# Linear attention plus GELU block: another order and other buffers for the attention denominator and the output stage

## The chip, the core and the metric

The kernel runs on one core of one Trainium2 chip. The metric is the device time of one execution in microseconds (us). Before the change the median of three runs is 207.69 us (207.5 to 208.19).

## What is computed

The input x has 2048 tokens of 640 features (D), in bf16. The result is x + A(LN(x)) + B(LN(x)). B is a GELU layer with 1536 hidden features. A is linear attention with 32 heads of 20 features:

```python
phi = lambda t: jnp.where(t > 0, t + 1, jnp.exp(t)) + 1e-6
pq, pk = phi(q), phi(k)
kv = jnp.einsum("bhsd,bhse->bhde", pk, v)
z = jnp.einsum("bhsd->bhd", pk)
num = jnp.einsum("bhqd,bhde->bhqe", pq, kv)
den = jnp.einsum("bhqd,bhd->bhq", pq, z)[..., None] + 1e-6
o = num / den
return (lambda x, *d: x.transpose(*d))(o, 0, 2, 1, 3).reshape(B, S, D) @ wo
```

The denominator `den` is one number for each token and head. This case is about when and by which engines it is computed.

## The kernel before

A planner records instructions for each of the five engines in the order in which the code is run, and works out the semaphore waits from what each instruction reads and writes. Every engine then executes its own list in order; an instruction that waits holds up all behind it on that engine. A DMA is an entry in the list of the engine that issues it, so a DMA that waits holds up that engine's later entries as well. Before the change all DMAs apart from two at the start are issued by SyncE (SP).

The tokens are 16 tiles of 128, in four chunks of four tiles. PSUM has eight banks, which `take` (L190) hands out in rotation; a matmul group that takes a bank waits until the reader of that bank's earlier content is done.

The stages, in order of TensorE's list:

1. Layer norm, the transposed xn and the hidden layer HG of B (L365), to about 60 us of the profile.
2. K for all tiles and phi (L502, `phi`, L481), then the product of xn with phi(K) (L535). Meanwhile VectorE sums phi(K) over tokens, which gives z.
3. Q in four chunks (`q_chunk`, L543). For each of five blocks j TensorE makes one bank of Q (L547), ScalarE takes its exponential into a rotating buffer `ek` of three (L489), and VectorE does two instructions, a minimum (L490) and a combination (L492), the second of which reads the bank and writes PQ. "phi" below means these two on VectorE, and the second is the eviction of the bank. Between chunks 0 and 1 stands a small product (L561). In chunk 2 two matmul groups "MT" (L579) follow each Q block; ScalarE copies them (L585), and SyncE issues a DMA transpose of the result into Msb (L587).
4. Output, tile by tile: an accumulation of 12 products with W2 (24 matmuls of 320 columns, "W2 part") and 5 products of PQ with Msb (10 matmuls, "M part") into a pair of banks (both L659); then VectorE adds the bias to x (`xb`, L633), adds the bank pair (L678), and SyncE stores the tile (L681). `out_w2` and `out_fin` make the two parts. The last tile (`out_last`) is made in three pieces of 320, 192 and 128 columns, each with its own addition (L698) and store (L701).

The denominator of a chunk goes through five steps. `den_part` (L590): VectorE adds up the five blocks of PQ weighted with z ("sums", one instruction for each block, L593 and L596). `den_gather` (L600): four DMAs of 64 KB bring four partition groups together. `den_inv` (L607): VectorE adds these and takes the reciprocal. `den_spread` (L614): four DMAs bring the reciprocals to all partitions. `rden_scale` (L621): VectorE multiplies the five blocks of PQ. Only after that may an M part of that chunk start. The buffers of these steps lie in the memory of xn_tm, which is no longer read by then.

Before the change the sums of chunk 0 stand in Q chunk 1, one after each phi; its inverse stands in Q chunk 2, after block 3's MT; its spread is issued between chunks 2 and 3. The output stage begins with the W2 parts of tiles 0 to 3; beside them VectorE scales chunk 0, makes the sums of chunks 1 and 2, and the inverse of chunk 1. Then come the M parts of tiles 0 to 3, with the scaling of chunk 1 behind tile 1, and from tile 4 on the W2 part and the M part of one tile directly after one another.

Of the kernel before, what the change touches and what calls it, by code (L numbers as in the profile page):

```python
# [5 lines left out]
ALU = AluOpType  # L6
ACT = mybir.ActivationFunctionType
P = 128
FP32 = mybir.dt.float32
BF16 = mybir.dt.bfloat16  # L10
# [102 lines left out]
def bass_parallel_sum__linear_attn_block__dense_activation_gelu__prompt_kernel(  # L113
    nc: bass.Bass, A_x, A_wqkv, A_wo, B_x, B_w1, B_b1, B_w2, B_b2, out):
    Batch, S, D = A_x.shape
    F = B_w1.shape[1]
    assert Batch == 1 and D == 640 and F % P == 0 and S % 512 == 0
    NT = S // P
    CH = 4
# [4 lines left out]
    H = 32  # L124
# [13 lines left out]
    with contextlib.ExitStack() as es:  # L138
# [36 lines left out]
        free = xn_tm[:].rearrange("p t d -> p (t d)")  # L175
        MH = P // H
        SW = CW // MH
        yv = [free[:, 2 * CW * i:2 * CW * (i + 1)].bitcast(FP32) for i in range(NC)]
        y4 = [free[:, 2 * CW * (NC + i):2 * CW * (NC + i + 1)].bitcast(FP32).rearrange("p (m s) -> p m s", m=MH)
              for i in range(NC)]  # L180
        rdv = [free[:, 4 * CW * NC + CW * i:4 * CW * NC + CW * (i + 1)] for i in range(NC)]
        den_sb = sb("den_sb", [P, 2, SW], FP32)
        rden = sb("rden", [P, 2, SW], BF16)
        out_sb = sb("out_sb", [P, 2, D], BF16)
# [43 lines left out]
        r_M = [R_("M%d" % j) for j in range(DT)]  # L228
        r_MT = [[R_("MT%d_%d" % (j, h)) for h in range(2)] for j in range(DT)]
        r_zsum, r_zhl, r_z = R_("zsum"), R_("zhl"), R_("z")  # L230
        r_y = [R_("y%d" % c) for c in range(NC)]
        r_y4 = [[R_("y4_%d_%d" % (c, q)) for q in range(4)] for c in range(NC)]
        r_rdb = [[R_("rdb%d_%d" % (c, q)) for q in range(4)] for c in range(NC)]
        r_den, r_rden = [R_("den0"), R_("den1")], [R_("rden0"), R_("rden1")]
        r_out = [R_("out0"), R_("out1")]
# [243 lines left out]


        def phi(src, b, nb, dst, res_dst, extra_w):  # L481
            s = ring_e[0] % 3
            ring_e[0] += 1
            w = D if nb == 2 else CW
            et = ek[:, s, 0:w]
            e2 = halves(et) if nb == 2 else et
            d2 = halves(dst) if nb == 2 else dst
            br = B_[b:b + nb]
            Pl.ins("scalar", lambda e: e.activation(e2, src, ACT.Exp), reads=br, writes=[r_ek[s]])  # L489
            Pl.ins(v, lambda e: e.tensor_scalar(et, et, 1.0, 1e-6, ALU.min, ALU.add),  # L490
                   reads=[r_ek[s]], writes=[r_ek[s]])
            Pl.ins(v, lambda e: e.scalar_tensor_tensor(out=d2, in0=src, scalar=0.0, in1=e2,  # L492
                                                       op0=ALU.max, op1=ALU.add),
                   reads=br + [r_ek[s]], writes=[res_dst] + extra_w)

        ring_e = [0]
        for t in range(NT):
# [45 lines left out]
        def q_chunk(c, after=None):  # L543
            cc = slice(c * CW, (c + 1) * CW)
            for j in range(DT):
                b = take(1)
                Pl.ins("tensor", [(lambda e, k=k, j=j, b=b: e.matmul(  # L547
                    bank(b), Wqkv[:, k, j:D:DT], xnT[:, k, cc],
                    start=(k == 0), stop=(k == DT - 1))) for k in range(DT)],
                    reads=[r_Wq] + r_xnT[c * CH:(c + 1) * CH], writes=[B_[b]])  # L550
                phi(bank(b), b, 1, PQ[:, j, cc], r_PQ[c][j], [])
                if after:
                    after(j)
# [36 lines left out]
        def den_part(c, j):  # L590
            pq = PQ[:, j, c * CW:(c + 1) * CW]
            if j == 0:
                Pl.ins(v, lambda e: e.tensor_scalar(yv[c], pq, z_sb[:, 0:1], 1e-6 / MH, ALU.mult, ALU.add),  # L593
                       reads=[r_z, r_PQ[c][0]], writes=[r_y[c]] + r_xn)
            else:
                Pl.ins(v, lambda e: e.scalar_tensor_tensor(out=yv[c], in0=pq, scalar=z_sb[:, j:j + 1], in1=yv[c],  # L596
                                                           op0=ALU.mult, op1=ALU.add),
                       reads=[r_z, r_PQ[c][j], r_y[c]], writes=[r_y[c]])

        def den_gather(c):  # L600
            for q in range(MH):
                dst = y4[c][H * q:H * (q + 1)]
                src = yv[c][:, SW * q:SW * (q + 1)]
                Pl.ins("sync", lambda e, dst=dst, src=src: e.dma_start(dst, src),  # L604
                       reads=[r_y[c]], writes=[r_y4[c][q]], dma=True)

        def den_inv(c):  # L607
            s = c % 2
            Pl.ins(v, lambda e: e.tensor_reduce(out=den_sb[:, s, :], in_=y4[c].rearrange("p m s -> p s m"),
                                                axis=mybir.AxisListType.X, op=ALU.add),  # L610
                   reads=r_y4[c], writes=[r_den[s]])
            Pl.ins(v, lambda e: e.reciprocal(rden[:, s, :], den_sb[:, s, :]), reads=[r_den[s]], writes=[r_rden[s]])

        def den_spread(c):  # L614
            for q in range(MH):
                dst = rdv[c][:, SW * q:SW * (q + 1)]
                src = rden[H * q:H * (q + 1), c % 2, :].unsqueeze(1).to_broadcast([H, MH, SW])
                Pl.ins("sync", lambda e, dst=dst, src=src: e.dma_start(dst, src),  # L618
                       reads=[r_rden[c % 2]], writes=[r_rdb[c][q]], dma=True)

        def rden_scale(c):  # L621
# [10 lines left out]
        def xb(t):  # L632
            Pl.ins(v, lambda e: e.tensor_tensor(out=x_res[:, t, :], in0=x_res[:, t, :], in1=b2bc[:], op=ALU.add),  # L633
                   reads=[r_xr[t // CH], r_b2], writes=[r_xb[t]])
# [2 lines left out]
            x_again(c)  # L637
        q_chunk(0)
        kvt_step()
        q_chunk(1, lambda j: den_part(0, j))  # L640
        den_gather(0)

        def mt_and_den(j):
            mt_block(j)
            if j == 3:
                den_inv(0)
        q_chunk(2, mt_and_den)
        den_spread(0)
        q_chunk(3)

        r_out3 = R_("out3")

        def mm_ops(t, i):
            tok = slice(t * P, (t + 1) * P)
# [17 lines left out]
        def out_fin(t, b):  # L672
            s = t % 2
            for i in range(JT, JT + DT):
                Pl.ins("tensor", [mm(b, t, i, 0), mm(b, t, i, 1)], reads=mm_reads(t, i), writes=B_[b:b + 2],
                       mark=(i == JT + DT - 1))
            xb(t)
            Pl.ins(v, lambda e: e.tensor_tensor(out=halves(out_sb[:, s, :]), in0=pair(b),  # L678
                                                in1=halves(x_res[:, t, :]), op=ALU.add),
                   reads=B_[b:b + 2] + [r_xb[t]], writes=[r_out[s]])  # L680
            Pl.ins("sync", lambda e: e.dma_start(ov[t * P:(t + 1) * P, :], out_sb[:, s, :]),  # L681
                   reads=[r_out[s]], dma=True)

        def out_last(t):
            xb(t)
            lo = 0
            for i, w in enumerate((HW, 3 * 64, P)):
                b = take(1)
                o = out_sb[:, (0, 1, 0)[i], (0, 0, HW)[i]:(0, 0, HW)[i] + w]
                hs = slice(lo, lo + w)  # L690
                lo += w
                fns = []
                for q in range(JT + DT):
                    l, r = mm_ops(t, q)
                    fns.append(lambda e, l=l, r=r, q=q, b=b, hs=hs, w=w: e.matmul(  # L695
                        bank(b, 0, w), l, r[:, hs], start=(q == 0), stop=(q == JT + DT - 1)))
                Pl.ins("tensor", fns, reads=[r for q in range(JT + DT) for r in mm_reads(t, q)], writes=[B_[b]])
                Pl.ins(v, lambda e, b=b, hs=hs, w=w, o=o: e.tensor_tensor(  # L698
                    out=o, in0=bank(b, 0, w), in1=x_res[:, t, hs], op=ALU.add),
                    reads=[B_[b], r_xb[t]], writes=[r_out3 if i == 2 else r_out[i]])  # L700
                Pl.ins("sync", lambda e, hs=hs, o=o: e.dma_start(ov[t * P:(t + 1) * P, hs], o),  # L701
                       reads=[r_out3 if i == 2 else r_out[i]], dma=True)

        n_sync = len(Pl.records["sync"])
        bs = [out_w2(t) for t in range(4)]
        rden_scale(0)
        for c in (1, 2):
            for j in range(DT):
                den_part(c, j)
            den_gather(c)  # L710
        den_inv(1)
        den_spread(1)
        for t in range(4):
            out_fin(t, bs[t])
            if t == 1:
                rden_scale(1)
        den_inv(2)
        den_spread(2)
        for t in range(4, NT - 1):
            b = out_w2(t)  # L720
            out_fin(t, b)
            if t == 4:
                for j in range(DT):
                    den_part(3, j)
                den_gather(3)
            elif t == 5:
                rden_scale(2)
                den_inv(3)
                den_spread(3)
            elif t == 8:  # L730
                rden_scale(3)
        out_last(NT - 1)

        stores = [ev for (waits, fns, ev, dma) in Pl.records["sync"][n_sync:] if dma]
        for ev in stores[:-1]:
            Pl.wait_event("gpsimd", ev)
        Pl.wait_event("sync", stores[-1])
# [36 lines left out]
```

## Time and profile before

| what | us |
|---|---|
| median of three runs | 207.69 |
| the profiled execution | 207.95 |
| its span, first to last instruction | 206.5 |
| TensorE busy | 200.3 (97%) |
| VectorE busy | 127.1 (62%) |
| ScalarE busy | 73.7 (36%) |
| Q chunks, start of chunk 0 to start of the first W2 part | 103.40 to 129.62 |
| first W2 part to the last tile's first matmul | 129.62 to 199.50 |

The granted TensorE clock is 1.000 over the span. In the profile's lines, PE is TensorE's matmuls, PEld its weight loads, DVE is VectorE, ACT is ScalarE, SP is SyncE; an engine's name with a q is its queue, where DMAs are issued. A timeline line has the start in us, the length in us (of the whole group where several are merged), the engine, the line of the code, the operation, the tile written and the tiles read, the count, and in brackets the idle time of the engine before it with what ended it. A line of the waits has the waiting instruction, what it waited for, the total in us, the number of times and the longest.

### The profile page before, as it was taken

To read this page: it belongs to the slowest core of one execution; us is meant where nothing else is said; L and a number is where in the kernel's file an instruction comes from. 1 tells how busy PE (TensorE), PEld (TensorE's weight loads), DVE (VectorE), ACT (ScalarE), POOL (GpSimd) and SP (SyncE) were. 2 spreads that over 40 slices of the span, in tenths; PEclk is the share of its full clock that TensorE was granted. 3 is DMA by queue.
4 is the path that set the end of the run, shared out by engine and by line. 5 is a ranking of instruction groups with operands and counts; after the bars stand their busy time and mean duration, and the time that the engine had idled before them with its cause. 6 is when DMAs were issued, how large, how long until landed. Compare 5 with 4: busy or idle time off the path is not lost.

```text
span 206.5 us, 3787 instructions
## 1 busy us (share of the span) xinstructions
PE 200.3 (97%) x1490; PEld 137.9 (67%) x1497; DVE 127.1 (62%) x247; ACT 73.7 (36%) x141; POOL 14.5 (7%) x43
## 2 busy tenths in 40 slices
PE   6999999999999999999999979999999999999995
PEld 1799987444457777777756535677757777777775
DVE  4777677100007888999288989698769976323322
ACT  3589887666676455111153666100000000000000
POOL 3143434300000000000000000000000000000000
DMA  6993745499930000000395016301312213100002
GB/s 175 364 348 69 76 89 93 84 364 267 300 125 0 0 0 3 0 0 3 67 334 172 3 51 126 61 0 51 80 64 76 82 58 107 39 35 32 32 35 64
DMA packets 30696, 20.28 MB, mean 98 GB/s; under 512 B 16262, under 2 KB 30678, under 8 KB 30678
## 3 DMA queue, kind: packets, MB, share of 16 engines
q1 hardware_dynamic: 30382, 19.77, 34.5%
q10 hardware_dynamic: 296, 0.27, 0.4%
q8 instruction: 12, 0.20, 0.4%
q14 instruction: 6, 0.05, 0.1%
HBM read 12.72 MB, written 2.62 MB: 74 GB/s over the span
## 4 chain that ended last, share of the span: by engine, by line
PE 76%; DVE 11%; DMA 6%; SPq 3%; issue 2%; DVEq 0%; ACT 0%
PE ps L365 24%; PE ps L659 23%; PE ps L535 11%; PE ps L502 11%; DMA xn_tm<-rden 3%; DVE xn_tm L596 3%; PE ps L547 3%; DVE PQ L492 2%; PE ps L695 2%; DMA xn_tm<-xn_tm 2%; SPq L618 2%; SPq L604 2%; PE ps L397 1%; DMA xPK<-in_A_x_dram 1%; DVE PQ L624 1%
## 5 line engine op out<-in xcount | busy, mean ns | idle before, releaser
L659 PE MATMUL ps<-W,HG 128*128 128x320 bf16 x360 | 50.9, 299 | 0.0
L365 PE MATMUL ps<-xnT,W 128*128 128x256 bf16 (+2 forms) x382 | 50.4, 293 | 0.2
L365 PEld LDWEIGHTS ps<-xnT,W 128*128 128x128 bf16 x385 | 33.9, 98 | 15.9
L659 PEld LDWEIGHTS ps<-W,HG 128*128 128x128 bf16 x360 | 35.2, 98 | 13.8
L369 ACT ACTIVATE HG<-ps,b1c 128x256 bf16<-128x256 f32 (+2 forms) x77 | 38.0, 516 | 12.7 <-PE ps L365 10.3
L489 ACT ACTIVATE ek<-ps 128x512 bf16<-128x512 f32 (+1 forms) x36 | 23.2, 645 | 19.3 <-PE ps L502 9.2
L490 DVE TENSOR_SCALAR ek<-ek 128x512 bf16<-128x512 bf16 (+1 forms) x36 | 10.9, 303 | 26.9 <-ACT ek L489 25.7
L678 DVE TENSOR_TENSOR out_sb<-ps,xPK 128x640 bf16<-128x640 f32 x15 | 12.4, 825 | 19.8 <-PE ps L659 17.2
L659 PE MATMUL ps<-Msb,PQ 128*128 128x320 bf16 x150 | 22.6, 299 | 0.2 <-DVE PQ L624 0.2
L547 PE MATMUL ps<-xnT,Wqkv 128*128 128x512 bf16 x96 | 22.2, 379 | 0.2
L502 PE MATMUL ps<-Wqkv,xnT 128*128 128x320 bf16 x160 | 21.9, 299 | 0.0
L535 PE MATMUL ps<-xPK,xn_tm 128*128 128x320 bf16 x160 | 21.9, 299 | 0.0
L502 PEld LDWEIGHTS ps<-Wqkv,xnT 128*128 128x128 bf16 x160 | 15.7, 98 | 6.2
L535 PEld LDWEIGHTS ps<-xPK,xn_tm 128*128 128x128 bf16 x160 | 15.7, 98 | 6.1
L659 PEld LDWEIGHTS ps<-Msb,PQ 128*128 128x128 bf16 x150 | 14.3, 98 | 6.7 <-DVE PQ L624 1.4
L547 PEld LDWEIGHTS ps<-xnT,Wqkv 128*128 128x128 bf16 x100 | 11.3, 118 | 8.5
L321 DVE BATCH_NORM_STATS2 stats<-xPK 128x6 f32<-128x320 bf16 x32 | 14.7, 470 | 2.7 <-DMA xPK<-in_A_x_dram 2.7
L492 DVE SCALAR_TENSOR_TENSOR PQ<-ps,ek 128x512 bf16<-128x512 f32 x20 | 13.8, 692 | 2.1
L492 DVE SCALAR_TENSOR_TENSOR xPK<-ps,ek 128x640 bf16<-128x640 f32 x16 | 13.2, 824 | 1.7
L596 DVE SCALAR_TENSOR_TENSOR xn_tm<-PQ,z_sb,xn_tm 128x512 f32<-128x512 bf16 x16 | 12.0, 749 | 0.4
L522 DVE TENSOR_TENSOR Msb<-Msb,xPK 128x640 f32<-128x640 f32 x14 | 11.6, 825 | 0.5
L331 POOL TENSOR_TENSOR rstd<-aggr,mhalf 128x1 f32<-128x1 f32 x16 | 9.1, 568 | 15.7 <-DVE aggr L329 15.7
(56 smaller groups left out, 95.4 us busy)
## 6 DMA issues: line engine op xcount, KB each, us to landing
xPK<-in_A_x_dram SPq DMA_DIRECT2D x6, 640.0 KB, 7.5
Wqkv<-in_A_wqkv_dram SPq DMA_DIRECT2D x3, 800.0 KB, 6.9
out_dram<-out_sb SPq DMA_DIRECT2D x15, 160.0 KB, 1.8
W<-in_B_w_dram SPq DMA_DIRECT2D x1, 1920.0 KB, 15.0
W<-in_B_w_dram SPq DMA_DIRECT2D x2, 640.0 KB, 7.1
xn_tm<-xn_tm SPq DMA_DIRECT2D x16, 64.0 KB, 2.2
Wo<-in_A_wo_dram SPq DMA_DIRECT2D x1, 750.0 KB, 11.8
xPK<-in_A_x_dram SPq DMA_DIRECT2D x4, 160.0 KB, 4.5
```

Of the source, the lines that this page charges most:

```text
L321: Pl.ins(v, lambda e: e.bn_stats(stats[:, s, 6 * h:6 * h + 6], x_in[:, t, h * HW:(h + 1) * HW]), reads=[r_x[t]], writes=[r_stats[s][h]])
L365: Pl.ins("tensor", [(lambda e, k=k: e.matmul(bank(b, 0, w), W1[:, k, jb * P:(jb + 1) * P], xnT[:, k, tok], start=(k == 0), stop=(k == DT - ...
L369: Pl.ins("scalar", lambda e: e.activation(HG[:, jb, tok], bank(b, 0, w), ACT.Gelu_apprx_tanh, bias=b1c[:, jb:jb + 1]), reads=[B_[b], r_b1c ...
L489: Pl.ins("scalar", lambda e: e.activation(e2, src, ACT.Exp), reads=br, writes=[r_ek[s]])
L492: Pl.ins(v, lambda e: e.scalar_tensor_tensor(out=d2, in0=src, scalar=0.0, in1=e2, op0=ALU.max, op1=ALU.add), reads=br + [r_ek[s]], writes= ...
L502: fns.append(lambda e, k=k, h=h, b=b, t=t: e.matmul(bank(b + h, 0, HW), xnT[:, k, t * P:(t + 1) * P], Wqkv[:, k, D + h * HW:D + (h + 1) * ...
L522: Pl.ins(v, lambda e, t=t: e.tensor_tensor(out=zsum, in0=zsum, in1=PK[:, t, :], op=ALU.add), reads=[r_PK[t], r_zsum], writes=[r_zsum])
L535: Pl.ins("tensor", [(lambda e, t=t, h=h, b=b, f=f: e.matmul(bank(b + h, 0, HW), xn_tm[:, t, f * P:(f + 1) * P], PK[:, t, h * HW:(h + 1) * ...
L547: Pl.ins("tensor", [(lambda e, k=k, j=j, b=b: e.matmul(bank(b), Wqkv[:, k, j:D:DT], xnT[:, k, cc], start=(k == 0), stop=(k == DT - 1))) fo ...
L596: Pl.ins(v, lambda e: e.scalar_tensor_tensor(out=yv[c], in0=pq, scalar=z_sb[:, j:j + 1], in1=yv[c], op0=ALU.mult, op1=ALU.add), reads=[r_z ...
L659: return lambda e: e.matmul(bank(b + h, 0, HW), l, r[:, h * HW:(h + 1) * HW], start=(i == 0), stop=(i == JT + DT - 1))
L678: Pl.ins(v, lambda e: e.tensor_tensor(out=halves(out_sb[:, s, :]), in0=pair(b), in1=halves(x_res[:, t, :]), op=ALU.add), reads=B_[b:b + 2] ...
```

## The change

Five edits, made together:

- phi in the Q chunks takes its exponential buffers from eight in the memory of xn_tm instead of the three of `ek`. The buffers of the sums and gathers shrink from four to two, used in turn by chunk.
- The sums of chunk 0 are made in Q chunk 2, one after each block's MT, instead of in chunk 1. The gather follows chunk 2, the inverse stands in chunk 3 after block 3, and the spread is issued after chunk 3.
- In the output stage the W2 part of tile t + 2 is put right behind the M part of tile t, from t = 2 on. The sums, inverses, spreads and scalings of chunks 1 to 3 get other places, and the bias additions of tiles 0 to 3 are made ahead of the inverse of chunk 1.
- Of the gathers and spreads of chunks 1 to 3, every second DMA is issued by ScalarE instead of SyncE.
- The last tile is written to a buffer `out_l` of its own, not to the two buffers that the tiles use in turn. At the end GpSimd waits for the output stores alone; the list had the gathers and spreads in it as well.

```diff
+        rdv = [free[:, CW * (8 + i):CW * (9 + i)] for i in range(NC)]
+        NEQ = 8
+        ekq = [free[:, CW * (12 + i):CW * (13 + i)] for i in range(NEQ)]
...
         def phi(src, b, nb, dst, res_dst, extra_w):
-            s = ring_e[0] % 3
+            if nb == 2:
+                s = ring_e[0] % 3
+                et, re = ek[:, s, :], r_ek[s]
+            else:
+                s = ring_e[0] % NEQ
+                et, re = ekq[s], r_ekq[s]
...
         def den_part(c, j):
             pq = PQ[:, j, c * CW:(c + 1) * CW]
             if j == 0:
-                Pl.ins(v, lambda e: e.tensor_scalar(yv[c], pq, z_sb[:, 0:1], 1e-6 / MH, ALU.mult, ALU.add),
-                       reads=[r_z, r_PQ[c][0]], writes=[r_y[c]] + r_xn)
+                Pl.ins(v, lambda e: e.tensor_scalar(yv[c % 2], pq, z_sb[:, 0:1], 1e-6 / MH, ALU.mult, ALU.add),
+                       reads=[r_z, r_PQ[c][0]], writes=[r_y[c % 2]])
...
+        def dma_q(c, q):
+            return "scalar" if c and q % 2 else "sync"
...
-                Pl.ins("sync", lambda e, dst=dst, src=src: e.dma_start(dst, src),
+                Pl.ins(dma_q(c, q), lambda e, dst=dst, src=src: e.dma_start(dst, src),
...
-        q_chunk(1, lambda j: den_part(0, j))
-        den_gather(0)
+        q_chunk(1)
 
         def mt_and_den(j):
             mt_block(j)
-            if j == 3:
-                den_inv(0)
+            den_part(0, j)
         q_chunk(2, mt_and_den)
+        den_gather(0)
+        q_chunk(3, lambda j: den_inv(0) if j == 3 else None)
         den_spread(0)
-        q_chunk(3)
...
+        out_l = sb("out_l", [P, D], BF16)
...
-            xb(t)
+            if t >= CH:
+                xb(t)
...
-                o = out_sb[:, (0, 1, 0)[i], (0, 0, HW)[i]:(0, 0, HW)[i] + w]
                 hs = slice(lo, lo + w)
+                o = out_l[:, hs]
...
         bs = [out_w2(t) for t in range(4)]
+        den_parts(1, 0, DT)
+        den_gather(1)
         rden_scale(0)
-        for c in (1, 2):
-            for j in range(DT):
-                den_part(c, j)
-            den_gather(c)
+        for t in range(CH):
+            xb(t)
         den_inv(1)
         den_spread(1)
-        for t in range(4):
+        den_parts(2, 0, 1)
+        out_fin(0, bs[0])
+        den_parts(2, 1, 2)
+        out_fin(1, bs[1])
+        rden_scale(1)
+        for t in range(2, NT - 1):
             out_fin(t, bs[t])
-            if t == 1:
-                rden_scale(1)
-        den_inv(2)
-        den_spread(2)
-        for t in range(4, NT - 1):
-            b = out_w2(t)
-            out_fin(t, b)
-            if t == 4:
-                for j in range(DT):
-                    den_part(3, j)
+            if t == 2:
+                den_parts(2, 2, DT)
+                den_gather(2)
+            elif t == 4:
+                den_inv(2)
+                den_spread(2)
+            elif t == 5:
+                den_parts(3, 0, DT)
                 den_gather(3)
-            elif t == 5:
+            elif t == 6:
                 rden_scale(2)
+            elif t == 7:
                 den_inv(3)
                 den_spread(3)
-            elif t == 8:
+            elif t == 9:
                 rden_scale(3)
+            if t + 2 < NT - 1:
+                bs.append(out_w2(t + 2))
         out_last(NT - 1)
```

`den_parts(c, lo, hi)` makes the sums of the blocks from lo to hi - 1 of chunk c.

## The prediction

> **What bounds the kernel now.** I read the page's busy row and its 40 slices first, then the waits of TensorE, then the timelines of TensorE, VectorE and SyncE around each wait, and last the end of the span. The page's rows for TensorE and its weight loads:
>
> ```profile
> PE 200.3 (97%) x1490; PEld 137.9 (67%) x1497; DVE 127.1 (62%) x247; ACT 73.7 (36%) x141; POOL 14.5 (7%) x43
> ...
> PE   6999999999999999999999979999999999999995
> ```
>
> TensorE is busy nearly all the time; after the first microseconds only slice 24 (118.7 to 123.9 us) and the last slice dip. So an edit in the attention denominator can gain only what TensorE loses to waits, plus something at the end. The waits of TensorE:
>
> ```profile
> PE ps L579 <- DVE PQ L492: 1.3, 1, 1.3
> ...
> PE ps L659 <- DVE PQ L624: 0.2, 1, 0.2
> ```
>
> The two left out lie before 7 us, which the change does not touch. These rows say 1.46 us. Here a rule of the Trainium skill speaks (Trainium Kernel Development and Optimization, Performance Expectations): matmul busy time is a bad metric, since matmuls are pipelined; weight-load busy is the better one. Weight loads at 67% would suggest a third of the span as room. The rows don't bear that out: 96 matmuls of 320 columns of the W2 stage start within 13.04 us (129.62 to 142.66), 136 ns each, and a load takes 98 ns of each interval, 72% with nothing idle. [...] I measure each from start to start. The timeline of TensorE:
>
> ```profile
> 121.38 0.23 PE L579 MATMUL ps<-W,Wo 120*128 120x120 bf16 x2 [1.29 <-DVE PQ L492]
> 121.45 1.25 PE L547 MATMUL ps<-xnT,Wqkv 128*128 128x512 bf16 x5
> 122.54 0.45 PE L579 MATMUL ps<-W,Wo 120*128 120x120 bf16 x6
> 122.84 1.25 PE L547 MATMUL ps<-xnT,Wqkv 128*128 128x512 bf16 x5
> ...
> 148.10 3.42 PE L659 MATMUL ps<-W,HG 128*128 128x320 bf16 x24
> 151.69 1.79 PE L659 MATMUL ps<-Msb,PQ 128*128 128x320 bf16 x10 [0.17 <-DVE PQ L624]
> 153.31 3.42 PE L659 MATMUL ps<-W,HG 128*128 128x320 bf16 x24
> 156.57 1.52 PE L659 MATMUL ps<-Msb,PQ 128*128 128x320 bf16 x10
> 157.93 3.42 PE L659 MATMUL ps<-W,HG 128*128 128x320 bf16 x24
> ```
>
> First wait, Q chunk 2: one step (a Q block and its two MT groups) takes 1.38 us undisturbed (Q blocks start at 116.97 and 118.35). The fourth Q block should start at 119.73 and starts at 121.45: **1.72 us** lost. Second, tile 4: W2 part to M part takes 3.59 instead of 3.26 us, and the M part 1.62 instead of 1.36: 0.33 + 0.26 = **0.59 us**.
>
> VectorE and ScalarE at the first wait:
>
> ```profile
> 118.88 0.69 DVE L492 SCALAR_TENSOR_TENSOR PQ<-ps,ek 128x512 bf16<-128x512 f32 x1
> 119.49 0.74 DVE L596 SCALAR_TENSOR_TENSOR xn_tm<-PQ,z_sb,xn_tm 128x512 f32<-128x512 bf16 x1
> ...
> 120.54 0.69 DVE L492 SCALAR_TENSOR_TENSOR PQ<-ps,ek 128x512 bf16<-128x512 f32 x1
> ```
>
> The banks rotate over 8. In chunk 2 each step takes three (Q, MT a, MT b), so MT b of step j takes the bank of Q block j-2, and MT a of step 2 that of chunk 1's last. These evictions end at 119.57 and 121.23, and TensorE goes on at 119.72 and 121.38, 0.15 us after each. VectorE is late because in chunk 1 it takes 1.66 us a step (113.51 to 115.17, phi plus a sum) while TensorE makes a Q block in 1.08.
>
> **The change, part by part.**
>
> *Sums of chunk 0 move from chunk 1 to chunk 2.* Chunk 1 is then phi alone: 1.00 us (121.14 to 122.14), inside TensorE's 1.08. So VectorE enters chunk 2 on time: chunk 1's last exp starts at 115.80, its eviction ends near 117.52, and the first exp of chunk 2 ends at 117.48. From 117.52 the steps take 1.40 with the first sum (112.11 to 113.51) and then 1.66; an eviction ends 1.08 after its step starts. Evictions of blocks 0, 1, 2 end at 118.6, 120.0, 121.66. MT b of steps 2, 3, 4 would like to start at 119.64, 121.02, 122.40 and may from 118.75, 120.15, 121.81. The narrowest slack is 0.59 us: the whole 1.72 us go. Bounds: a sum at its full 0.74 instead of 0.66 us moves the last by 0.16, still nothing; if chunk 2's steps (ScalarE copying MT from PSUM beside them, a mix that no row shows with sums) cost 0.4 more, the loss is about 0.3. A gain beyond 1.72 is excluded, as nothing but that wait is there. I take 1.72, range 1.4 to 1.72.
>
> *Eight exp buffers in Q.* ScalarE's waits for a buffer are 0.5 us in all, one time, and TensorE doesn't wait for them. VectorE will end chunk 2 at 117.52 + 1.40 + 4 x 1.66 = 125.56, some 2 us behind, less than the three steps that three buffers cover. 0 either way.
>
> *Chunk 0's gather, inverse, spread come later.* SyncE: the five transposes of chunk 2 (1.23 us each) are now ahead of the gather; the last is ready near 123.8, issued by 125.1, so they hold nothing. Gather from 125.6, landing 4.2 later (120.26 to 124.45): 129.8. VectorE meanwhile does four phis of chunk 3 to 129.6, waits 0.2, and takes 2.03 for the inverse (124.57 to 126.60): 131.9. The fifth phi waits behind it, to 132.9; its bank is wanted by W2 of tile 3 at 137.7 at the earliest, so that hides it. Spread: 5.1 us from inverse to landing (146.02 to 151.11): 137.0. The sums of chunk 1 (3.55, 136.12 to 139.67) run to 136.45 beside it, and the scaling of chunk 0 (1.77) ends at 138.8. The M part of tile 0 is due at 129.62 - 1.72 + 13.04 = 140.94. Cover 2.1 us: 0 lost, range 0 to 0.5.
>
> *Head of the output stage.* Behind that VectorE has four bias additions (0.53 each) to 140.9, the inverse of chunk 1 to 142.95, one sum (0.41), then the first output addition (0.82) to 144.2. M parts of tiles 0 to 2 take 3 x 1.36, so W2 of tile 4, in tile 0's banks, is due at 145.02: slack 0.8. This is the tightest place of the new order. Scaling of chunk 1: spread from 142.95, landing 148.05 at the latest, done 149.8; its first reader, the M part of tile 4, is due at 145.02 + 3.26 + 1.36 + 3.26 = 152.9, because W2 parts now stand ahead. So the 0.59 us go. Same sum for chunk 2: done near 166, wanted at 171.4; chunk 3: near 180, wanted at 190. 0 lost; range 0 to 1.
>
> *Gather and spread on two queues.* Each issue takes 0.60 us of SyncE's time, so two fewer behind one another save 1.2 of a gather's 4.2 us. A rule of the Trainium skill (DMA: Bandwidth & Descriptors, Issuing engines are not separate DMA queues) is against hoping for more: all issues run on the same DMA engines and interleave, only issue time is saved. By the row alone chunk 1's gather lands at 136.5 + 3.0 = 139.5; if interleaving ate even that, 140.7. VectorE is at its additions until 140.9, so the sum gets 0 from either. ScalarE's own issues (0.62 and 0.41 at the start) lie where it has no other work.
>
> *Own buffer for the last tile.* The timeline of the end:
>
> ```profile
> 204.06 0.33 SPq L701 DMA_DIRECT2D out_dram<-out_sb  x1
> ...
> 204.36 0.29 DVE L698 TENSOR_TENSOR out_sb<-ps,xPK 128x128 bf16<-128x128 f32 x1
> ...
> 204.91 0.43 SPq L701 DMA_DIRECT2D out_dram<-out_sb  x1
> ```
>
> The waits put 2.6 us before the first two of the three additions to tile 14's store, but the third still starts when TensorE ends. The cost is on SyncE: the last store issues at 204.91, though its data is there at 204.65 and an issue follows some 0.1 later. Without the pile: 204.75, so **0.15 us**; bounds 0 and 0.25. GpSimd's final waits are now for output stores alone: 0, since it ends with the stores as before.
>
> Sum: 1.72 + 0.59 + 0.15 = 2.46 us. The profiled execution took 207.95 us (span 206.5): 205.49. The median of the runs, 207.69, lies 0.26 lower, so 205.2.
>
> **The rivals.**
>
> *Part of the wait comes back* (VectorE slower in chunk 2, or the first output addition late): for it speaks the 0.59 and 0.8 of slack, less than one phi; against it that all durations are of the same shapes. Up to 1.4 us lost: 205.6 to 206.6.
>
> *The change doesn't do what it says in chunk 2*: the weight load's wait is put to ScalarE's MT copies (1.43), and if those were the cause the 1.72 stays: 207.69 - 0.74 = 206.95. The copies end by 119.3, long before 121.34, while both restarts follow an eviction by 0.15: unlikely.
>
> *Slower: the inverse of chunk 1 blocks VectorE.* It stands ahead of tile 0's addition in VectorE's order and waits for the gather on two queues. If that lands late, the addition, tile 0's banks and W2 of tile 4 all slip by it. It costs from 140.9 + 0.8 = 141.7 on, and makes the kernel slower once it eats the 2.46 as well, at 144.2: 7.7 us after its issue, against 4.2 in the trace. At 9 us: 207.69 + 1.3 = 209. For it: no gather on ScalarE's queue is in the trace. Against: that queue's start-up load of 256 KB landed in 4.0 us, and the DMA engines are 17% busy in this stretch (129.6 to 142.6).
>
> **How the numbers follow.** A measurement of this kernel tells about 0.3%, 0.6 us, from no change. The forecast, 205.2 (204.8 to 205.6): 0.70. Part of the wait back: 0.10. The first wait stays: 0.05, of which I count 0.03 as faster. Slower: 0.11. Cancelling losses within 0.6 us: 0.04. Faster 0.83, same 0.06, slower 0.11. The range takes the first two: 204.7 to 206.6.
>
> **What would show it.** TensorE's row for MT waiting on L492 is gone and chunk 2 keeps its 1.38 us a step; W2 begins near 127.9; every W2 part follows its M part at 3.26 and 1.36 us; the waits of the scalings are VectorE's alone; the last store issues within 0.15 us of the last addition. I am wrong if TensorE shows a new wait on an output addition (tile 4), on a scaling (tile 0), or if MT still waits in chunk 2.

## The result, and the profile after

The changed kernel takes 205.34 us (median of 4 runs, 205.16 to 205.5), where the kernel before took 207.81 in runs beside it (207.5 to 208.19). The ratio is 0.988, with a 95% interval of 0.986 to 0.990: 2.5 us less, with 2.46 forecast. The profiled execution took 205.16 us, its span is 203.8 us, and the granted TensorE clock is 1.000 as before.

The page's busy row and the slices of TensorE:

```profile
PE 200.1 (98%) x1497; PEld 138.4 (68%) x1497; DVE 126.9 (62%) x247; ACT 73.5 (36%) x141; POOL 14.5 (7%) x43
...
PE   7899999999999999999999999999999999999996
```

The busy times are those of before: no work went away. The dip that stood in slice 24 is gone. The waits of TensorE are down to these two, both before 6 us:

```profile
PE ps L311 <- DVE warm L281: 1.3, 1, 1.3
PE ps L389 <- DVE xn_tm L382: 0.6, 1, 0.6
```

The timeline of TensorE shows the places of both waits. L585 is the MT group, L553 the Q block, L669 the output stage:

```profile
120.80 0.45 PE L585 MATMUL ps<-W,Wo 120*128 120x120 bf16 x6
121.10 1.25 PE L553 MATMUL ps<-xnT,Wqkv 128*128 128x512 bf16 x5
122.19 0.45 PE L585 MATMUL ps<-W,Wo 120*128 120x120 bf16 x6
122.48 5.57 PE L553 MATMUL ps<-xnT,Wqkv 128*128 128x512 bf16 x25
127.88 13.20 PE L669 MATMUL ps<-W,HG 128*128 128x320 bf16 x96
140.92 4.24 PE L669 MATMUL ps<-Msb,PQ 128*128 128x320 bf16 x30
145.00 3.42 PE L669 MATMUL ps<-W,HG 128*128 128x320 bf16 x24
148.26 1.52 PE L669 MATMUL ps<-Msb,PQ 128*128 128x320 bf16 x10
```

Read the starts. The last Q block of chunk 2 starts at 121.10 and the first of chunk 3 at 122.48, 1.38 later, an undisturbed step. W2 begins at 127.88 instead of 129.62: 1.74 us. Three M parts then take 4.08, a W2 part 3.26, and no start in the stage is late. The last tile begins at 197.16 instead of 199.50, 2.34 us earlier, so the second wait gave 0.60. The timelines of SyncE and VectorE at the end:

```profile
201.46 0.33 SPq L712 DMA_DIRECT2D out_dram<-out_l  x1
...
202.02 0.29 DVE L709 TENSOR_TENSOR out_l<-ps,xPK 128x128 bf16<-128x128 f32 x1 [0.59 <-PE ps L706]
...
202.34 0.33 SPq L712 DMA_DIRECT2D out_dram<-out_l  x1
```

The last store is issued 0.03 us after its data is there (202.31), where it was 0.26 before, and the issue takes 0.33 instead of 0.43. From the end of the last addition to the end of the span it is 1.49 us instead of 1.85: 0.36. The three terms, 1.74 + 0.60 + 0.36, are the 2.7 us between the spans (206.5 and 203.8) of these two executions; the medians differ by 2.5.

### The profile page after: what moved, and what is told of

Same layout as the page of the kernel before. It is cut to its first block, busy times and chain, and to the rows that moved or that the text cites. A ratio compares the mean times of both kernels' runs of the same rounds, so it can differ in the third digit from the quotient of the medians.

```text
span 203.8 us, 3769 instructions
## 1 busy us (share of the span) xinstructions
PE 200.1 (98%) x1497; PEld 138.4 (68%) x1497; DVE 126.9 (62%) x247; ACT 73.5 (36%) x141; POOL 14.5 (7%) x43
## 4 chain that ended last, share of the span: by engine, by line
PE 96%; DVE 1%; DMA 1%; issue 0%; DVEq 0%
PE ps L669 34%; PE ps L368 25%; PE ps L541 11%; PE ps L508 11%; PE ps L553 11%; PE ps L706 2%; PE ps L400 1%; DMA xPK<-in_A_x_dram 1%; DVE stats L324 1%; PE ps L567 1%; PE ps L585 1%; PE ps L389 0%; PE ps L352 0%; DVE xn_tm L382 0%; DVE out_l L709 0%
## 5 line engine op out<-in xcount | busy, mean ns | idle before, releaser
L669 PE MATMUL ps<-W,HG 128*128 128x320 bf16 x360 | 50.9, 299 | 0.0
L669 PEld LDWEIGHTS ps<-W,HG 128*128 128x128 bf16 x360 | 35.2, 98 | 13.8
L553 PE MATMUL ps<-xnT,Wqkv 128*128 128x512 bf16 x100 | 22.8, 379 | 0.0
L669 PE MATMUL ps<-Msb,PQ 128*128 128x320 bf16 x150 | 22.3, 299 | 0.0
L496 DVE TENSOR_SCALAR ek<-ek 128x640 bf16<-128x640 bf16 x16 | 5.2, 325 | 26.0 <-ACT ek L495 24.8
L669 PEld LDWEIGHTS ps<-Msb,PQ 128*128 128x128 bf16 x150 | 14.7, 98 | 5.7
L553 PEld LDWEIGHTS ps<-xnT,Wqkv 128*128 128x128 bf16 x100 | 11.3, 118 | 8.5
L495 ACT ACTIVATE xn_tm<-ps 128x512 bf16<-128x512 f32 x20 | 11.9, 597 | 9.4 <-PE ps L553 8.7
L498 DVE SCALAR_TENSOR_TENSOR PQ<-ps,xn_tm 128x512 bf16<-128x512 f32 x20 | 13.8, 692 | 2.1
L495 ACT ACTIVATE ek<-ps 128x640 bf16<-128x640 f32 x16 | 11.3, 704 | 9.2 <-PE ps L508 9.2
```

Source lines behind the costliest of these rows:

```text
L553: Pl.ins("tensor", [(lambda e, k=k, j=j, b=b: e.matmul(bank(b), Wqkv[:, k, j:D:DT], xnT[:, k, cc], start=(k == 0), stop=(k == DT - 1))) fo ...
L669: return lambda e: e.matmul(bank(b + h, 0, HW), l, r[:, h * HW:(h + 1) * HW], start=(i == 0), stop=(i == JT + DT - 1))
```

## The experiments

Each ran in five rounds beside the kernel before. Ratios are to that kernel.

**One part alone: the sums of chunk 0 in chunk 2.** On the kernel before:

```diff
-        q_chunk(1, lambda j: den_part(0, j))
-        den_gather(0)
+        q_chunk(1)
 
         def mt_and_den(j):
             mt_block(j)
-            if j == 3:
-                den_inv(0)
+            den_part(0, j)
         q_chunk(2, mt_and_den)
+        den_gather(0)
+        q_chunk(3, lambda j: den_inv(0) if j == 3 else None)
         den_spread(0)
-        q_chunk(3)
```

> The kernel before with one part alone: chunk 0's sums in Q chunk 2, its gather behind chunk 2, its inverse in chunk 3 and its spread behind it; three exp buffers, one queue, the old output stage. My theory (TensorE's waits follow VectorE's order): the first wait goes, W2 begins 1.74 us earlier, at 127.9. But in the old output stage VectorE then scales chunk 0 to 138.1, makes ten sums to 145.3, gets chunk 1's gather near 146.0, and does tile 0's addition only near 149.3, where W2 of tile 4 is due at 146.4: 3.1 us lost there, and about 1.2 more at the M part of tile 4 for chunk 1's scaling, in place of 0.59 before. Sum: -1.74 + 4.3 - 0.59 = +2.0, so 209.8 us, slower. Rival (the parts add up, each with its own gain): 207.8 - 1.7 = 206.1 us.

Measured: 209.72 us, ratio 1.0088 (1.0055 to 1.0122). Slower, near my 209.8. Three of the six runs had a granted clock of 0.992; the median of the other three is 209.64, so the clock is not the cause. The timeline of TensorE of this kernel, at full clock:

```profile
127.92 13.20 PE L658 MATMUL ps<-W,HG 128*128 128x320 bf16 x96
140.96 5.60 PE L658 MATMUL ps<-Msb,PQ 128*128 128x320 bf16 x40
148.98 3.43 PE L658 MATMUL ps<-W,HG 128*128 128x320 bf16 x24 [2.43 <-DVE out_sb L677]
153.11 1.78 PE L658 MATMUL ps<-Msb,PQ 128*128 128x320 bf16 x10 [0.69 <-DVE PQ L624]
154.73 3.42 PE L658 MATMUL ps<-W,HG 128*128 128x320 bf16 x24
```

W2 does begin 1.7 us earlier, and all of it is lost again at tile 4. Its W2 part would be due at 140.96 + 4 x 1.36 = 146.40 and starts at 148.98: 2.58 lost. Its M part comes 4.13 later instead of 3.26 and takes 1.62 instead of 1.36: 1.13 more. Together 3.71, where this tile lost 0.59 before: 3.12 more, less the 1.7 won, so TensorE comes out 1.4 us behind the old trace, less than the 2.0 that I had put together. (This execution was the fastest of the six.) The timeline of VectorE tells why:

```profile
136.07 1.77 DVE L624 TENSOR_TENSOR PQ<-PQ,xn_tm 128x512 bf16<-128x512 bf16 x5 [3.09 <-DMA xn_tm<-rden]
137.75 0.48 DVE L593 TENSOR_SCALAR xn_tm<-PQ,z_sb 128x512 f32<-128x512 bf16 x1
138.27 3.11 DVE L596 SCALAR_TENSOR_TENSOR xn_tm<-PQ,z_sb,xn_tm 128x512 f32<-128x512 bf16 x4
141.30 0.48 DVE L593 TENSOR_SCALAR xn_tm<-PQ,z_sb 128x512 f32<-128x512 bf16 x1
141.82 3.11 DVE L596 SCALAR_TENSOR_TENSOR xn_tm<-PQ,z_sb,xn_tm 128x512 f32<-128x512 bf16 x4
145.63 1.03 DVE L609 TENSOR_REDUCE den_sb<-xn_tm 128x128 f32<-128x512 f32 x1 [0.70 <-DMA xn_tm<-xn_tm]
146.70 0.95 DVE L612 RECIPROCAL rden<-den_sb 128x128 bf16<-128x128 f32 x1
147.57 0.43 DVE L633 TENSOR_TENSOR xPK<-xPK,b2bc 128x640 bf16<-128x640 bf16 x1
148.10 0.82 DVE L677 TENSOR_TENSOR out_sb<-ps,xPK 128x640 bf16<-128x640 f32 x1
```

The scaling of chunk 0, ten sums, an inverse that waits for its gather and a bias addition stand ahead of tile 0's addition, which alone frees the banks for W2 of tile 4. It ends at 148.92. The same list stood there in the kernel before, with this addition:

```profile
146.47 0.82 DVE L678 TENSOR_TENSOR out_sb<-ps,xPK 128x640 bf16<-128x640 f32 x1
```

It ended at 147.29, 0.81 before W2 of tile 4 started at 148.10. With the sums in chunk 2 that list begins 1.6 later, as its scaling waits for a later spread (136.07 instead of 134.44), and TensorE comes 1.7 earlier. The parts of the change do not add up: this one pays only with the other order behind it.

**The new output stage alone**, on the kernel before, all DMAs on SyncE: the diff of the change from `bs = [out_w2(t) ...]` on, and the bias additions. Core:

```diff
         bs = [out_w2(t) for t in range(4)]
+        den_parts(1, 0, DT)
+        den_gather(1)
         rden_scale(0)
-        for c in (1, 2):
-            for j in range(DT):
-                den_part(c, j)
-            den_gather(c)
+        for t in range(CH):
+            xb(t)
         den_inv(1)
         den_spread(1)
...
```

> The kernel before with the new output stage alone (places of sums, inverses, spreads, scalings and bias additions, W2 parts two tiles ahead), all DMAs on SyncE, chunk 0's sums still in chunk 1. My theory: the first wait of 1.72 us stays, the second of 0.59 us goes: 207.2 us. Rival (the new order only pays behind an early W2 start, or one queue makes chunk 1's spread late): 207.8 us or above, with a wait of W2 or M of tile 4 in the trace.

Measured: 207.34 us, ratio 0.9966 (0.9948 to 0.9985), 0.3 to 1.1 us less. In its trace the 1.29 us wait of MT stands as before and W2 begins at 129.56; from there to the M part of tile 5 no start is late. The 0.6 us of the second wait are this part's own.

**The last tile's buffer alone**, on the kernel before:

```diff
+        out_l = sb("out_l", [P, D], BF16)
...
-                o = out_sb[:, (0, 1, 0)[i], (0, 0, HW)[i]:(0, 0, HW)[i] + w]
                 hs = slice(lo, lo + w)
+                o = out_l[:, hs]
...
```

> The kernel before with the last tile's own buffer alone. The two traces give 0.26 us from the last data to the issue of the last store before and 0.03 after, and an issue of 0.43 before and 0.33 after, so 0.15 to 0.33 us: 207.5 to 207.65. Rival (the final waits of GpSimd or the landing set the end): no change, 207.8.

Measured: 207.88 us, ratio 1.0001 (0.9981 to 1.0021). The runs can't tell 0.3 us, and can't exclude it. The trace has the effect: 1.55 us from the end of the last addition (204.85) to the end of the span (206.4), against 1.85 before. But in this profile TensorE reaches the last tile at 199.70 instead of 199.50, from a later start of work that the edit doesn't touch: the first MT starts at 116.94 instead of 116.68, and over the traces of all runs at 116.63 to 117.08. Such shifts between executions are as large as the term. So the 0.3 us are seen in traces, and not shown in times.

**The W2 parts not two tiles ahead**, on the kernel after:

```diff
         for t in range(2, NT - 1):
+            if t >= 4:
+                bs.append(out_w2(t))
             out_fin(t, bs[t])
...
-            if t + 2 < NT - 1:
-                bs.append(out_w2(t + 2))
```

> The kernel after, but the W2 part of tile t from 4 on directly ahead of its own M part, as before the change; the places on VectorE, SyncE and ScalarE relative to the M parts unchanged. My theory now: VectorE's order is what ended the wait at tile 4. Chunk 1's scaling ends at 146.7, and the M part of tile 4 would be due at 149.6 in this order too: no wait, 205.3 us. Rival, as the prediction put it (the W2 parts that stand ahead cover the scaling): the wait comes back in part, up to 0.6 us, 205.9 us.

Measured: 205.57 us, ratio 0.9885 (0.9857 to 0.9913); no difference from the kernel after that the runs can tell. The timelines of TensorE and VectorE of this kernel:

```profile
146.41 3.42 PE L669 MATMUL ps<-W,HG 128*128 128x320 bf16 x24
149.66 1.52 PE L669 MATMUL ps<-Msb,PQ 128*128 128x320 bf16 x10
151.02 3.42 PE L669 MATMUL ps<-W,HG 128*128 128x320 bf16 x24
```

```profile
144.99 1.76 DVE L633 TENSOR_TENSOR PQ<-PQ,xn_tm 128x512 bf16<-128x512 bf16 x5 [0.24 <-DMA xn_tm<-rden]
```

The M part of tile 4 is due 3.3 us earlier than in the kernel after, at 149.66, and starts then: chunk 1's scaling is done at 146.75. The old order of TensorE loses nothing. What ended the second wait is VectorE's order in the output stage; in the kernel with the first part alone, which keeps the old order there, the wait grew to 1.13.

**All DMAs on SyncE**, on the kernel after:

```diff
-            return "scalar" if c and q % 2 else "sync"
+            return "sync"
```

> The kernel after with all gathers and spreads issued by SyncE. My theory: each gather and spread of chunks 1 to 3 lands up to 1.2 us later, and VectorE has other work or TensorE has slack (W2 of tile 4 due at 145.0, tile 0's addition done at 143.3; chunk 1's scaling done at 146.7, wanted at 152.9): no change, 205.3 us. Rival (the second queue is needed, chunk 1's inverse delays tile 0's addition): more than 205.9 us, and a wait of W2 of tile 4.

Measured: 205.32 us, ratio 0.9877 (0.9857 to 0.9896). No change, as expected. The timeline of VectorE shows what the second queue did buy:

```profile
141.17 1.04 DVE L618 TENSOR_REDUCE den_sb<-xn_tm 128x128 f32<-128x512 f32 x1 [0.99 <-DMA xn_tm<-xn_tm]
142.24 0.95 DVE L621 RECIPROCAL rden<-den_sb 128x128 bf16<-128x128 f32 x1
143.11 0.39 DVE L599 TENSOR_SCALAR xn_tm<-PQ,z_sb 128x512 f32<-128x512 bf16 x1
143.41 0.82 DVE L689 TENSOR_TENSOR out_sb<-ps,xPK 128x640 bf16<-128x640 f32 x1
```

VectorE waits 0.99 us for chunk 1's gather. Tile 0's addition ends at 144.23, W2 of tile 4 starts at 145.42 in this trace, on time: the delay comes out of the slack.

**Three exp buffers**, on the kernel after:

```diff
-                s = ring_e[0] % NEQ
-                et, re = ekq[s], r_ekq[s]
+                s = ring_e[0] % 3
+                et, re = ek[:, s, 0:CW], r_ek[s]
```

> The kernel after with the three exp buffers of before in the Q chunks. My theory: VectorE is never three steps behind, ScalarE waits little and TensorE not at all: 205.3 us. Rival (the exp buffers are what let TensorE pass chunk 2): W2 begins later than 127.9, up to 207.0 us.

Measured: 205.51 us, ratio 0.9894 (0.9867 to 0.9921). W2 begins at 127.86, as with eight.

**More work for VectorE in chunk 2**, on the kernel after; the second sum's output is not used:

```diff
             den_part(0, j)
+            pq = PQ[:, j, 2 * CW:3 * CW]
+            Pl.ins(v, lambda e: e.scalar_tensor_tensor(out=yv[1], in0=pq, scalar=z_sb[:, j:j + 1], in1=yv[0],
+                                                       op0=ALU.mult, op1=ALU.add),
+                   reads=[r_z, r_PQ[2][j], r_y[0]], writes=[r_y[1]])
```

> The kernel after with extra work: in chunk 2 VectorE makes each sum a second time into a buffer whose content is not used (0.66 us a step). It tests the two slacks of the sum. My theory: evictions of blocks 1 and 2 end 0.66 and 1.32 later, the latter at 122.95, so MT of step 4, due at 122.40, may start at 123.1: 0.7 us lost in chunk 2. VectorE then is 3.4 us later at the head of the output stage; tile 0's addition ends at 146.45, W2 of tile 4 is due at 145.8: some 0.8 lost there. Together 206.9 us. Rival (TensorE is held by ScalarE's copies or by nothing of VectorE's in chunk 2): 205.3 us; rival (no slack at all, every extra microsecond of VectorE counts): 205.3 + 3.3 = 208.6 us.

Measured: 207.91 us, ratio 1.0014 (0.9997 to 1.0031): 1.0 us more than I had expected, and between both rivals. The timelines of VectorE and TensorE, L655 being the second sum:

```profile
119.92 0.29 DVE L496 TENSOR_SCALAR xn_tm<-xn_tm 128x512 bf16<-128x512 bf16 x1
...
120.92 0.74 DVE L602 SCALAR_TENSOR_TENSOR xn_tm<-PQ,z_sb,xn_tm 128x512 f32<-128x512 bf16 x1
121.77 0.75 DVE L655 SCALAR_TENSOR_TENSOR xn_tm<-PQ,z_sb,xn_tm 128x512 f32<-128x512 bf16 x1
122.44 0.28 DVE L496 TENSOR_SCALAR xn_tm<-xn_tm 128x512 bf16<-128x512 bf16 x1
122.84 0.69 DVE L498 SCALAR_TENSOR_TENSOR PQ<-ps,xn_tm 128x512 bf16<-128x512 f32 x1
```

```profile
122.34 0.38 PE L585 MATMUL ps<-W,Wo 120*128 120x120 bf16 x4
123.68 0.23 PE L585 MATMUL ps<-W,Wo 120*128 120x120 bf16 x2 [0.96 <-ACT W L591]
123.75 5.85 PE L553 MATMUL ps<-xnT,Wqkv 128*128 128x512 bf16 x24
129.44 13.20 PE L673 MATMUL ps<-W,HG 128*128 128x320 bf16 x96
142.48 4.24 PE L673 MATMUL ps<-Msb,PQ 128*128 128x320 bf16 x30
147.60 3.43 PE L673 MATMUL ps<-W,HG 128*128 128x320 bf16 x24 [0.89 <-DVE out_sb L693]
```

The mechanism is as stated, the size of the dose was off. A step takes 2.52 us (119.92 to 122.44) instead of 1.66, so 0.86 more and not 0.66: the second sum reads what the first has just written, and starts 0.85 after it (120.92 to 121.77). The eviction of block 2 ends at 123.53, and MT of step 4 goes on at 123.68, 0.15 later, as in the kernel before. From MT's start to the next Q block it is 1.41 us instead of 0.29: 1.12 lost. Chunk 3 takes 5.69 instead of 5.40, 0.29 lost, which I had not foreseen: its third block takes the bank of chunk 2's fourth, whose eviction ends at 126.05, and starts at 126.20, again 0.15 later. W2 of tile 4 comes 5.12 after the M part of tile 0 instead of 4.08, 1.04 lost. The sum is 2.45; the spans differ by 2.6, and this trace was 0.16 later before chunk 2's first MT already (116.82 to 116.66). The wait is put down to ScalarE's copy (L591), which ends about then too, but by the rotation MT b of step 4 waits for block 2's bank, which that copy does not read. One extra instruction a step uses up the slack at both places and gives the whole gain back.

**Without three of the edits**, on the kernel after: the diffs of the W2 parts, of SyncE and of the three exp buffers, together.

> The kernel after without three of its edits at once: three exp buffers, all DMAs on SyncE, and the W2 part of tile t from 4 on directly ahead of its own M part. What is left of the change: the place of chunk 0's sums, VectorE's order in the output stage, the last tile's buffer. My theory: these carry all of the gain: 205.3 us, no wait of TensorE after 6 us. Rival (the three cover for each other, each alone was dispensable only because the others were there): 205.9 us or more, with a wait at W2 or M of tile 4.

Measured: 205.78 us, ratio 0.9876 (0.984 to 0.9911). No wait of TensorE after 6 us, and a span of 203.9. The three don't cover for one another. VectorE's wait for chunk 1's gather is there (0.99 us), and its scaling ends at 148.66, before the M part of tile 4 starts, on time, at 149.67.

**Other pieces of the last tile**, on the kernel after, as an attempt at more:

```diff
-            for i, w in enumerate((HW, 3 * 64, P)):
+            for i, w in enumerate((HW, 4 * 64, 64)):
```

> The kernel after with the last tile's pieces of 320, 256 and 64 columns instead of 320, 192 and 128. TensorE no longer waits, so the end is what is left: from TensorE's last matmul to the end of the span 1.8 us, of which the last addition is 0.29 (0.36 with 192 columns, so about 0.1 for each 128). My theory: the addition of 64 columns takes some 0.05 less and the 17 matmuls of 64 columns can't start faster than every 56 ns as those of 128 do, as a weight load stands ahead of each, which costs 17 x 27 ns = 0.45: 205.7 us. Rival (a matmul of 64 columns starts every 29 ns): 205.25 us.

Measured: 205.87 us, ratio 0.9885 (0.9849 to 0.9921); no gain, and my reason was wrong. The timelines of TensorE and SyncE:

```profile
201.62 0.51 PE L706 MATMUL ps<-W,HG 128*128 128x64 bf16 x12
201.97 0.31 PE L706 MATMUL ps<-Msb,PQ 128*128 128x64 bf16 x5
```

```profile
202.27 0.33 SPq L712 DMA_DIRECT2D out_dram<-out_l  x1
```

Twelve matmuls of 64 columns start within 0.35 us, 29 ns each, so TensorE doesn't lose the 0.45 us that I had expected. But the second piece's store is issued at 202.27, and the third's stands behind it on SyncE until 202.65, 5.20 us after the last tile began (197.45). With 128 columns it was issued 5.18 after (197.16 to 202.34). What the smaller addition gave, SyncE's issue took.

## Why the prediction was right

*The first wait.* Forecast 1.72, measured 1.74. VectorE's evictions in chunk 2 of the kernel after:

```profile
117.89 0.69 DVE L498 SCALAR_TENSOR_TENSOR PQ<-ps,xn_tm 128x512 bf16<-128x512 f32 x1
...
119.28 0.69 DVE L498 SCALAR_TENSOR_TENSOR PQ<-ps,xn_tm 128x512 bf16<-128x512 f32 x1
...
120.94 0.69 DVE L498 SCALAR_TENSOR_TENSOR PQ<-ps,xn_tm 128x512 bf16<-128x512 f32 x1
```

Those of blocks 0, 1, 2 end at 118.58, 119.97 and 121.63, where the sum had 118.6, 120.0 and 121.66; W2 begins at 127.88 (127.9). That it was the eviction two blocks back is shown by the extra work: 0.86 us more a step brings the wait back, with the same 0.15 us between eviction and matmul.

*The second wait.* Forecast 0.59, measured 0.60. But I credited it to the wrong edit, so that the number came out is in part luck. The step "because W2 parts now stand ahead" failed: with the W2 parts at their old place nothing waits. VectorE's order carries it: the sums of chunk 1 stand ahead of chunk 0's scaling, and those of chunk 2 no longer ahead of chunk 1's inverse. Chunk 1's scaling in the kernel before:

```profile
151.21 1.77 DVE L624 TENSOR_TENSOR PQ<-PQ,xn_tm 128x512 bf16<-128x512 bf16 x5 [2.58 <-DMA xn_tm<-rden]
```

It starts at 145.03 in the kernel after. Which of the two moves would have been enough was not run. My own sum held the answer: chunk 1's scaling at 149.8 at the latest, with its first blocks before that, against an M part due at 149.6 in the old order.

*The tightest place.* It was named rightly, W2 of tile 4 behind tile 0's addition, and mis-sized: the addition ends at 143.30, not 144.2, so the slack is 1.7 us and not 0.8. VectorE there:

```profile
139.90 1.03 DVE L618 TENSOR_REDUCE den_sb<-xn_tm 128x128 f32<-128x512 f32 x1
...
142.48 0.82 DVE L689 TENSOR_TENSOR out_sb<-ps,xPK 128x640 bf16<-128x640 f32 x1 [0.25 <-PE ps L669]
```

Two terms were too dear. From chunk 0's inverse to its scaling it is 4.4 us (131.98 to 136.39), not 5.1, and the scaling stands directly behind the sums of chunk 1, so the spread took no longer than that: where VectorE does wait for it, in the first part alone, it is 4.0 (132.03 to 136.07). And four bias additions in a row take 0.42 each, not 0.53, which was the start of one to the start of the addition behind it.

*The end.* Forecast 0.15 with a bound of 0.25; the traces show 0.3 (1.85 to 1.55 and to 1.49). The mechanism was right, SyncE's pile of three issues. Two sizes were off: a free issue follows its data by 0.03 and not by some 0.1 (the first of the pile showed it, 204.03 to 204.06), and an issue in the pile also takes longer, 0.43 instead of 0.33. The 2.6 us of the waits stand once, before the first of the three additions. The times can't confirm a term of this size. GpSimd's shorter list of final waits was not run alone; the buffer without it has 0.30 of the 0.36.

*Edits costed at nothing* were nothing, eight exp buffers and two queues, and so were the W2 parts ahead, which I had credited with the second wait; singly and together. The second queue saves VectorE a wait that was covered: chunk 1's inverse starts 3.40 us after the gather's first issue with two queues (136.50 to 139.90) and 4.25 with one (136.92 to 141.17). These 0.85 us are less than the 1.2 of issue time that the row gave. They fit the rule of the Trainium skill (DMA: Bandwidth & Descriptors, Issuing engines are not separate DMA queues) that a second issuing engine saves issue time only. The dearer reading, that interleaving eats even that (140.7), did not come true.

*The rivals.* No part of the first wait came back: no row of TensorE shows it. "The change doesn't do what it says" is refuted by the trace. The slower case, VectorE blocked ahead of tile 0's addition, did not occur here, but its place is real: the sums moved alone make the kernel 1 to 2.5 us slower there. I had given it a late DMA as the only cause; the order of VectorE's own work is the nearer one.

*The sum.* That 2.46 meets the 2.47 between the medians so closely is luck: the terms add up to 2.70 in the traces, 0.21 of the difference lies at the end, and executions differ by more than that.

## What to carry to other kernels

When TensorE is at its limit everywhere but at two short waits, follow the bank or buffer that each wait is for back to the instruction that frees it, and ask what stands ahead of that instruction on its in-order engine; the named releaser may be another. Moving work off one such place puts it ahead of the next bank release, so lay out VectorE's whole list with durations and check every due time of TensorE: here one move alone cost 1.9 us, and with the rest of the list rearranged the same move gave 1.7. Edits whose cover is another edit's slack should be run alone and left out together; three of these could be dropped.

## What the runs showed of the hardware

- A VectorE sum that reads what the sum just ahead wrote starts after that one's length of 0.74 to 0.75 us: 0.79 later where it writes the same buffer (133.36 to 134.15 in the kernel after), 0.85 later with the extra sum, which writes another (120.92 to 121.77). An instruction that doesn't read it starts before that length is over, 0.67 later (121.77 to 122.44 in the same trace). Why 0.79 and 0.85 differ is not shown.
- Matmuls of 64 columns start every 29 ns, those of 128 every 56 ns (12 from 200.87 to 201.54 in the kernel after), each with its own weight load, whose length is 98 ns.
- An issue of chunk 1's gather takes 0.77 us on ScalarE (two in 1.54) and 0.63 on SyncE (two in 1.26, both at 136.50 in the kernel after); over all gathers of that trace the medians are 0.75 and 0.61.
